# A fifth Winograd pair in blocks 3 to 6 of an attention and GEGLU kernel

## Chip, cores and metric

The kernel runs on one core of one Trainium2 chip. The metric is the device time of one launch, in microseconds; lower is better. The time before is the median of three runs.

## What is computed

The reference is linear attention followed by a gated feed-forward layer, in float32. With 8 batches, 8 heads, 576 positions and a head width of 64 it is, cut to what matters:

```python
q_s = softmax(q, axis=-1)                 # over the 64 of a head
k_s = softmax(k, axis=2)                  # over the 576 positions
kv  = einsum('bhsd,bhse->bhde', k_s, v)
x   = einsum('bhsd,bhde->bhse', q_s, kv)  # then heads side by side: 4608 x 512
g, val = x @ w_gate, x @ w_val            # 512 -> 1536 each
out = (gelu(g) * val) @ w_out             # 1536 -> 512
```

## The kernel before, in words

**Blocks.** The 576 rows of a batch are 512 main rows and 64 that are left over. Blocks 0 to 7 are the main rows of the eight batches; block 8 is the 8 x 64 left-over rows together. The order is 0 to 6, then 8, then 7. While block b runs through the feed-forward layer, the attention of block b+1 is fitted in, and loads go two blocks ahead. Tensors are float16 on TensorE; everything in PSUM is float32.

**Feed-forward of a block.** The hidden layer is twelve tiles of 128 columns, 0 to 11. A tile needs a gate and a value product: eight matmuls of 512 columns when done plainly. In the plain form (`half`) the steps are called `10g` and `10v`: after `g` ScalarE takes a Gelu of the PSUM bank (L625), after `v` VectorE multiplies it in (L627) and writes the tile of `ht`.

**Pairs.** From block 2 on, some tiles are computed in pairs k and k+3 with seven half-size products in place of eight (Winograd's form of Strassen's product): 28 matmuls of 256 columns for two tiles. `pair_step` cuts a pair into four steps, `k.1` to `k.4`, over three PSUM banks `pa`, `pb`, `pc`:

- `k.1`: product 1 into `pa`, which ScalarE copies to `pb` (L663); product 5 into `pc`, of which a scaled copy is taken (ScalarE L643; in blocks 7 and 8 VectorE L641).
- `k.2`: product 6 onto `pa`, of which ScalarE takes a copy (L643); product 3 onto `pc`; VectorE adds `pc` and the copy of `pa` into `cc` (L647).
- `k.3`: product 7 onto `pa`; VectorE adds `pa` and the copy of `pc` into `cc` (L647); product 2 onto `pb`, finished by `final` (ScalarE L633, VectorE L634); `upper` ends the other half: Gelu on ScalarE (L651), product on GpSimd (L653).
- `k.4`: product 4 onto `pa` and its `final`.

Since a product is put onto a bank in place, `k.2` on TensorE waits for the copies of `k.1`, `k.3` for the copy of `pa`, and `k.4` for the add of `pa` in `k.3`. A `final` is issued one pair step late where the next step is a `.1`. The buffer `cc` has two places, which the pairs take by turns from block 3 on.

**Sums.** The pairs need sums of weights (`sum_wgv`, L587, four for the gate and four for the value weights) and of x (`sum_x`, L593, GpSimd). The argument k = 6 of `sum_wgv` is pair 6, 7 is pair 7 and 8 is pair 8, and n says for how many pairs one instruction works; sum 3 is made in place. The output product is a Winograd product too (`out_strassen`, `product`, L718, seven products over tiles 0 to 5 and 6 to 11), with sums of `ht` (`sum_h`, L576): sums 1 to 4 for j = 0, 1, 2.

**Order.** Nothing reorders instructions; each engine follows the order that is written. For blocks 2 and up it is a string of steps: `THREE` for block 2, `FOUR` for blocks 3 to 6, `SIX` for 8 and 7. Letters run what the table `plan` holds under them (`ride`): `a`, `n`, `m` normalise q of the next block (VectorE L240 and L242, GpSimd L250), `l` loads, `t` is a DMA transpose, `s0`, `u0`, `s1`, `u1` are sums of `ht`, and `w`, `x` in block 2 are sums of weights. Step `2.4` comes inside `out_strassen`, after three tiles of its product 1. The points `NS` 0 to 4 in `out_strassen` run the attention of the next block, casts of v, and sums of weights. In this function VectorE also takes copies of PSUM (L750) and adds (L756).

Of the kernel before, what the change touches and what calls it, by code (L numbers as in the profile page):

```python
# [18 lines left out]
def kernel(  # L19
# [12 lines left out]
    B, H, S, D = q.shape  # L32
# [16 lines left out]
    NO = NFI // 2  # L49
# [30 lines left out]
    def big(shape, dt, name, hold=False, seed=False):  # L80
        tag = ring.pop(next(i for i, x in enumerate(ring) if x in full) if seed else 0)
        t = ps_big.tile(shape, dt, name=name, tag=tag)
        words = 1
        for n in shape[1:]:
            words *= n
        (full.add if words == 512 and shape[0] == 128 and dt == f32 else full.discard)(tag)
        if hold:
            held[id(t)] = (t, tag)
        else:
            ring.append(tag)  # L90
        return t

    def let_go(t):
        ring.append(held.pop(id(t))[1])
# [26 lines left out]
    for i, nm in enumerate("gv"):  # L121
        n = 3 * NO * P
# [472 lines left out]
    def product_gv(i, ps, xt, k, first):  # L595
# [3 lines left out]
        for t, w, nm in ((0, wv_sb, "v"), (1, wg_sb, "g")):  # L599
            ss = ws[(nm, k // NO)]  # L600
            for c in range(2):
# [7 lines left out]


    THREE = ("a 6g l 6v 0.1 9g 0.2 9v w 0.3 7g 0.4 n m 1.1 t 7v 1.2 10g 1.3 s0 10v 1.4 2.1 u0 8g 2.2 8v"
             " 2.3 s1 11g u1 2.4 11v x")
    FOUR = ("a 7g l 7v n 0.1 6.1 0.2 6.2 0.3 6.3 m 10g 0.4 6.4 1.1 t 10v 1.2 s0 8g u0 1.3 8v 1.4 2.1"
            " 11g s1 2.2 11v 2.3")
    SIX = ("0.1 6.1 0.2 6.2 0.3 6.3 0.4 1.1 6.4 7.1 s0 1.2 7.2 1.3 u0 7.3 1.4 2.1 7.4 8.1 2.2"
           " 8.2 2.3 s1 8.3 2.4")
    steps = {b: (SIX if b >= B - 1 else THREE if b == 2 else FOUR).split() for b in range(2, B + 1)}
    live = {}

    def half(b, xt, c, nm):  # L620
# [87 lines left out]
    def product(i, ps, first, ts=(0, 1), js=range(NO)):  # L708
        for j in js:
            for t in ts:  # L710
                c0, c1 = slice(t * P, (t + 1) * P), slice(256 + t * P, 256 + (t + 1) * P)
                a = {1: ht[:, j, c0], 2: ht[:, NO + j, c0], 3: s4[:, j, c0], 4: ht[:, NO + j, c1],
                     5: sh[1][:, j, c0], 6: sh[2][:, j, c0], 7: ht[:, j, c1]}[i]
                w = {1: wo_sb[:, j, 0:256], 2: wo_sb[:, NO + j, 0:256],
                     3: wo_sb[:, NO + j, 256:512]}.get(i)
                if w is None:
                    w = tw[{4: 4, 5: 1, 6: 2, 7: 3}[i]][:, j]
                nc.tensor.matmul(ps[t], a, w, start=(first and j == js[0] and (  # L718
                    t == ts[0] or ps[t].tensor is not ps[ts[0]].tensor)),
                                 stop=(j == js[-1]), skip_group_check=True)  # L720

    def get_x(b):
        return get_xt(b) if b < B else xtr

    def last_js(b):
        return (NO - 2 if b < 2 else NO // 2 - 1, NO)

    def out_strassen(b, last):
        yo = [yop.tile([P, 2, C], f32, name="yo", tag="yo") for _ in range(2)]
        c = (slice(0, 256), slice(256, 512))  # L730
        ps, tiles_ = {}, {}

        def get(nm):
            if last:
                tiles_[nm] = [big([P, 256], f32, "ps" + nm, True) for _ in range(2)]
                ps[nm] = [x for x in tiles_[nm]]
            else:
                tiles_[nm] = [big([P, 2, 256], f32, "ps" + nm, True)]
                ps[nm] = [tiles_[nm][0][:, t] for t in range(2)]

        def parts(nm):
            return [(0, ps[nm][0]), (1, ps[nm][1])] if last else [(slice(0, 2), tiles_[nm][0])]

        def snap(nm, act=False):
            sn = ffn.tile([P, 2, 256], f32, name="sn", tag="gl")
            for n, (t, src) in enumerate(parts(nm)):
                if n or act:
                    nc.scalar.activation(out=sn[:, t], in_=src, func=ACTF.Copy, scale=1.0 / _H_SCALE)
                else:
                    nc.vector.tensor_scalar(out=sn[:, t], in0=src, scalar1=1.0 / _H_SCALE,  # L750
                                            scalar2=None, op0=ALU.mult)
            return sn

        def add(nm, sn, half, col):
            for t, src in parts(nm):
                nc.vector.scalar_tensor_tensor(  # L756
                    out=yo[half][:, t, c[col]], in0=src, scalar=1.0 / _H_SCALE,
                    in1=sn[:, t], op0=ALU.mult, op1=ALU.add)

        js = (0, 1, 2, 3, 4, 5) if b < 2 else (0, 3, 1, 4, 2, 5)  # L760
        get("a")
        four = 2 < b < B - 1
        cut = 3 if four else 4
        product(1, ps["a"], True, js=js[:cut])
        if four:
            pair_step(b, get_x(b), NO // 2 - 1, 4)
            product(1, ps["a"], False, js=js[cut:4])
        ride(b, NS, 0)
        if four:
            ride(b, PR, "u1")  # L770
        if b >= B - 1:
            pair_step(b, get_x(b), NFI - NO // 2 - 1, 4)
        get("b")
        product(1, ps["a"], False, js=js[4:])
        if b > 1:
            s1 = snap("a", True)
        ride(b, PR, "e")
        sum_h(*last_js(b), (1,))
        if b >= B - 1:
            ride(b, PR, "u1")  # L780
        sum_h(*last_js(b), (2,))
        if b < 2:
            s1 = snap("a")
        product(2, ps["b"], True, js=js)
        add("b", s1, 0, 0)
        for x in tiles_["b"]:
            let_go(x)
        sum_h(*last_js(b), (4,), "pool" if b > 1 else "dve")
        get("c")
        product(5, ps["c"], True, js=js)  # L790
        sum_h(*last_js(b), (3,), "pool" if b > 1 else "dve")
        s5 = snap("c", b == B or b == B - 2)
        ride(b, NS, 1)
        product(6, ps["a"], False, js=js)
        s2 = snap("a", b == B or b == B - 2)
        ride(b, NS, 2)
        cut = NO - 1 if 1 < b < B - 2 else NO
        product(3, ps["c"], False, js=js[:cut])
        if cut < NO:
            product(7, ps["a"], False, js=js)  # L800
            add("a", s5, 1, 1)
            product(3, ps["c"], False, js=js[cut:])
        add("c", s2, 0, 1)
        for x in tiles_["c"]:
            let_go(x)
        store_rows(b, 0, yo[0])
        if last:
            finish_last(b, ps["a"], yo[1], s5)
            return
        if cut == NO:  # L810
            product(7, ps["a"], False, js=js)
            add("a", s5, 1, 1)
        ride(b, NS, 4)
        if b == B:
            go_on(B - 1, get_x(B - 1), 1)
        product(4, ps["a"], False, js=js)
        nc.scalar.activation(out=yo[1][:, :, c[0]], in_=tiles_["a"][0], func=ACTF.Copy,
                             scale=1.0 / _H_SCALE)
        let_go(tiles_["a"][0])
        store_rows(b, 1, yo[1])  # L820
# [97 lines left out]
    FI, NS, PR = range(3)  # L918
    plan = {}

    def at(b, kind, i, *fns):
        plan.setdefault((b, kind, i), []).extend(fns)

    L = lambda f, *a: (lambda: f(*a))
# [40 lines left out]
    for b in range(2, B):  # L965
        n = b + 1
# [13 lines left out]
    for b in range(2, B - 1):  # L980
        n = b + 1
# [6 lines left out]
    for b in range(2, B + 1):  # L988
        for j in range(NO // 2 - 1):
            at(b, PR, f"s{j}", L(sum_h, j, NO, (1,)))  # L990
            if j and b >= B - 1:
                at(b, PR, f"u{j}", L(sum_h, j, NO, (2, 3, 4)))
            else:
                at(b, PR, f"s{j}", L(sum_h, j, NO, (3,), "pool"))
                at(b, PR, f"u{j}", L(sum_h, j, NO, (2,)), L(sum_h, j, NO, (4,), "pool"))
    for i, xs_ in (("w", ("g1", "v1", "g2", "v2")), ("x", ("g4", "v4", "g3", "v3"))):
        for x in xs_:
            at(2, PR, i, L(sum_wgv, x[0], int(x[1]), NO, 1, "pool"))
    for b, i, x in ((3, 2, "g1"), (3, 2, "g2"), (4, 2, "v1"), (4, 2, "v2"), (6, 1, "g4"), (6, 1, "v4"),
                    (6, 2, "g3"), (6, 2, "v3")):  # L1000
        at(b, NS, i, L(sum_wgv, x[0], int(x[1]), NO + 1, 2))


    def ride(b, kind, i):
        for fn in plan.get((b, kind, i), []):
            fn()
# [63 lines left out]
```

## Time and profile before

| | |
|---|---|
| median of three runs | 293.6 us (293.58 to 293.72) |
| the profiled execution: time, span | 293.74 us, 292.0 us |
| TensorE busy | 282.8 us, 97% of the span |
| VectorE, ScalarE, GpSimd busy | 221.8, 194.9, 200.5 us |
| block 2 | 82.0 to 112.45 us of the span |
| blocks 3, 4, 5, 6 | 30.02, 30.08, 30.07, 30.28 us each |

The blocks are cut where the first matmul of a block's feed-forward part starts. The share of TensorE says that it is the engine to look at; whether it waits anywhere is read from its timeline. A row of the timeline has the start in us, the time, the engine, the line and operation, output and inputs, the count, and the wait ahead of it with what ended it. Instructions on ScalarE and VectorE overlap a little: the next one can start some 0.1 us ahead of the end that the row gives.

### The profile page before, as it was taken

The page shows a single profiled execution, that of the slowest core. Times are in us where ns is not written, and L with a number is a line of the kernel's source. Part 1 is how long each engine was busy: PE and PEld are TensorE (multiplying, and loading weights), DVE is VectorE, ACT ScalarE, POOL GpSimd, SP SyncE. Part 2 cuts the span into 40 slices and gives each one's busy share as a digit, 9 for nine tenths or more (in the row PEclk, how much of TensorE's full clock was granted, in tenths as well). Part 3 has the DMA queues.
Part 4 walks back from the last instruction along what each step waited for, and adds up shares of the span by engine and source line. Part 5 has one row for each costly group of instructions (what it writes and reads, how often), then busy time and mean ns, then how long its engine had stood idle before and what let it go on. Part 6 is the DMA issues. An engine that isn't in the chain of part 4 may idle for free.

```text
span 292.0 us, 6352 instructions
## 1 busy us (share of the span) xinstructions
PE 282.8 (97%) x2449; PEld 203.1 (70%) x2449; DVE 221.8 (76%) x412; ACT 194.9 (67%) x322; POOL 200.5 (69%) x187
## 2 busy tenths in 40 slices
PE   3999999999999999999999999999999999999994
PEld 1544446445866687778776878687868888888883
DVE  2854789878878768677967897687868879938992
ACT  3773367785786578758986798669864577537650
POOL 1567846970489799877888688869895576283640
PEclk9999999999999999999999999999999999999999
DMA  6999999998059704990299019901141110033003
GB/s 215 374 381 388 401 391 390 357 342 237 4 175 387 160 3 144 356 221 3 114 341 283 3 74 326 318 6 74 73 77 26 72 74 0 3 72 75 0 2 144
DMA packets 54622, 51.72 MB, mean 177 GB/s; under 512 B 18496, under 2 KB 50496, under 8 KB 54592
## 3 DMA queue, kind: packets, MB, share of 16 engines
q1 hardware_dynamic: 52864, 49.49, 53.5%
q10 hardware_dynamic: 1728, 1.84, 2.0%
q8 instruction: 19, 0.31, 0.4%
q14 instruction: 11, 0.09, 0.1%
HBM read 37.75 MB, written 9.44 MB: 162 GB/s over the span
## 4 chain that ended last, share of the span: by engine, by line
PE 94%; DVE 2%; DMA 2%; ACT 0%; issue 0%; ACTq 0%
PE pga L606 19%; PE psa L718 15%; PE psg L467 14%; PE psv L467 14%; PE pgc L606 9%; PE psc L718 7%; PE pgb L606 5%; PE psb L718 4%; PE psy L535 4%; DMA qt<-in_q_dram 2%; PE pskv L343 2%; PE psx L430 1%; DVE rq L240 1%; PE psx L409 1%; DVE eq L250 0%; PE pskv L284 0%
## 5 line engine op out<-in xcount | busy, mean ns | idle before, releaser
L467 PE MATMUL psg<-xt,wg_sb 128*128 128x512 f16 x184 | 49.3, 379 | 0.0
L467 PE MATMUL psv<-xt,wv_sb 128*128 128x512 f16 x184 | 49.2, 379 | 0.0
L250 POOL TENSOR_TENSOR eq<-eq,rrq 128x640 f16<-128x640 f16 (+1 forms) x27 | 34.7, 1303 | 11.8 <-DVE rrq L242 8.2
L718 PEld LDWEIGHTS <-ht 128*128 128x128 f16 x384 | 36.6, 98 | 7.6 <-issue 2.5
L606 PEld LDWEIGHTS <-wv_sb 128*128 128x128 f16 x248 | 24.1, 98 | 9.4 <-issue 1.0
L467 PEld LDWEIGHTS <-wv_sb 128*128 128x128 f16 x184 | 17.9, 98 | 18.0 <-issue 0.8
L653 POOL TENSOR_TENSOR ht<-eq 128x512 f16<-128x512 f32 x14 | 17.8, 1273 | 18.1 <-ACT eq L651 18.1
L467 PEld LDWEIGHTS <-wg_sb 128*128 128x128 f16 x184 | 17.9, 98 | 16.5
L576 POOL TENSOR_TENSOR s<-ht,sh 128x512 f16<-128x512 f16 x19 | 22.4, 1178 | 9.8 <-DVE sh L576 9.8
L634 DVE SCALAR_TENSOR_TENSOR ht<-pga,glq 128x256 f16<-128x256 f32 x31 | 13.1, 423 | 20.7 <-ACT glq L633 20.6
L188 POOL CAST v<-vt 128x640 f16<-128x640 f32 x26 | 18.7, 761 | 12.8 <-PE pskv L343 11.3
L576 POOL TENSOR_TENSOR ht<-ht 128x512 f16<-128x512 f16 x19 | 23.1, 1215 | 6.1 <-DVE sh L576 6.1
L606 PEld LDWEIGHTS <-wg_sb 128*128 128x128 f16 x248 | 24.2, 98 | 2.8
L653 POOL TENSOR_TENSOR ht<-cc 128x512 f16<-128x512 f32 x15 | 19.5, 1303 | 8.5 <-ACT cc L651 8.5
L472 ACT ACTIVATE gl<-psg 128x512 f32<-128x512 f32 x24 | 13.8, 598 | 16.7 <-PE psg L467 16.7
L633 ACT ACTIVATE glq<-pgb 128x256 f32<-128x256 f32 x31 | 11.7, 379 | 18.7 <-PE pgb L606 10.9
L718 PE MATMUL psa<-tw,ht 128*128 128x256 f16 x192 | 23.4, 272 | 0.1
L473 DVE SCALAR_TENSOR_TENSOR ht<-psv,gl 128x512 f16<-128x512 f32 x24 | 16.1, 688 | 9.5 <-PE psv L467 7.6
L212 ACT ACTIVATE ek<-kt 128x1280 f16<-128x1280 f32 (+1 forms) x11 | 19.1, 1748 | 5.5 <-DMA kt<-in_k_dram 3.9
L663 ACT COPY pgb<-pga 128x512 f32<-128x512 f32 x31 | 18.0, 580 | 6.7 <-PE pga L606 6.4
L643 ACT ACTIVATE snq<-pga 128x512 f32<-128x512 f32 x31 | 18.5, 600 | 4.0 <-PE pga L606 3.7
L240 DVE TENSOR_REDUCE rq<-eq 128x20 f32<-128x1280 f16 (+1 forms) x12 | 17.2, 1432 | 4.6 <-ACT eq L212 4.6
(172 smaller groups left out, 729.6 us busy)
## 6 DMA issues: line engine op xcount, KB each, us to landing
out_dram<-yo SPq DMA_DIRECT2D x15, 512.0 KB, 3.4
kt<-in_k_dram SPq DMA_DIRECT2D x7, 640.0 KB, 9.0
vt<-in_v_dram SPq DMA_DIRECT2D x7, 640.0 KB, 5.3
qt<-in_q_dram SPq DMA_DIRECT2D x7, 640.0 KB, 7.7
qt<-in_q_dram SPq DMA_DIRECT2D x8, 512.0 KB, 7.8
wost<-in_moe_w_out_dram SPq DMA_DIRECT2D x6, 512.0 KB, 7.9
kt<-in_k_dram SPq DMA_DIRECT2D x6, 512.0 KB, 9.5
vt<-in_v_dram SPq DMA_DIRECT2D x6, 512.0 KB, 5.8
```

What stands on the lines that cost most here:

```text
L188: nc.gpsimd.tensor_copy(out=dst, in_=src)
L212: nc.scalar.activation(out=dst[:, n0:NC, h0 * D:h1 * D].rearrange(o, d=D, **({"t": 2} if b >= QUAD else {})), in_=heads(tiles[(nm, b)], b, ...
L240: nc.vector.reduce_sum(rq, e, axis=mybir.AxisListType.X)
L250: (nc.gpsimd if eng == "pool" else nc.vector).tensor_tensor(out=e, in0=e, in1=rrq.unsqueeze(-1).to_broadcast((P, n, 2, D)), op=ALU.mult)
L467: nc.tensor.matmul(ps, w[:, ci, fi * P:(fi + 1) * P], xt[:, ci, :], start=(ci == 0), stop=(ci == HP - 1))
L473: nc.vector.scalar_tensor_tensor(out=ht[:, fi, :], in0=psv, scalar=_H_SCALE, in1=gl, op0=ALU.mult, op1=ALU.mult)
L576: (nc.gpsimd if eng == "pool" else nc.vector).tensor_tensor(out=o, in0=a, in1=b, op=op)
L606: nc.tensor.matmul(ps[:, t], a, x, start=(first and t == 0 and c == 0), stop=(c == 1), skip_group_check=True)
L643: nc.scalar.activation(out=sn, in_=ps, func=ACTF.Copy, scale=_H_SCALE)
L653: (nc.vector if k == NFI - NO // 2 - 1 else nc.gpsimd).tensor_tensor(out=ht[:, k:k + NO // 2 + 1:NO // 2, 256:512], in0=cc[:, :, 0], in1=c ...
L663: nc.scalar.copy(out=pb, in_=pa)
L718: nc.tensor.matmul(ps[t], a, w, start=(first and j == js[0] and (t == ts[0] or ps[t].tensor is not ps[ts[0]].tensor)), stop=(j == js[-1]), ...
```

## The change

Blocks 3 to 6 get pair 7, so tiles 7 and 10 are no longer done plainly in them; the string is now called `FIVE`, and pair 7 takes turns with pair 1. Tiles 8 and 11 stay plain. The sums of weights for pair 7, four for the gate and four for the value, are made together with those for pair 6 in block 2 (n = 2), on VectorE where it was GpSimd, four at `w` and two each at `NS` 1 and 2. The later sums, spread over blocks 3, 4, 5 and 6, are for pair 8 alone (n = 1). In blocks 3 to 6 the sums 2, 3 and 4 of `ht` for j = 1 are all on VectorE, in `out_strassen` behind sum 1 of j = 2; before, sum 3 was on GpSimd at `s1`, and sum 2 on VectorE and sum 4 on GpSimd stood ahead of bank `b`.

```diff
     THREE = ("a 6g l 6v 0.1 9g 0.2 9v w 0.3 7g 0.4 n m 1.1 t 7v 1.2 10g 1.3 s0 10v 1.4 2.1 u0 8g 2.2 8v"
-             " 2.3 s1 11g u1 2.4 11v x")
-    FOUR = ("a 7g l 7v n 0.1 6.1 0.2 6.2 0.3 6.3 m 10g 0.4 6.4 1.1 t 10v 1.2 s0 8g u0 1.3 8v 1.4 2.1"
-            " 11g s1 2.2 11v 2.3")
+             " 2.3 s1 11g u1 2.4 11v")
+    FIVE = ("a 8g l 8v n 0.1 6.1 0.2 6.2 0.3 6.3 m 0.4 1.1 6.4 7.1 t 1.2 s0 7.2 1.3 u0 7.3 2.1 1.4 11g 2.2"
+            " 7.4 s1 11v 2.3")
...
-        if four:
-            ride(b, PR, "u1")
...
         sum_h(*last_js(b), (1,))
-        if b >= B - 1:
+        if b > 2:
             ride(b, PR, "u1")
...
-            if j and b >= B - 1:
+            if j and b > 2:
                 at(b, PR, f"u{j}", L(sum_h, j, NO, (2, 3, 4)))
...
-    for i, xs_ in (("w", ("g1", "v1", "g2", "v2")), ("x", ("g4", "v4", "g3", "v3"))):
+    for kind, i, xs_ in ((PR, "w", ("g1", "v1", "g2", "v2")), (NS, 1, ("g4", "v4")), (NS, 2, ("g3", "v3"))):
         for x in xs_:
-            at(2, PR, i, L(sum_wgv, x[0], int(x[1]), NO, 1, "pool"))
-    for b, i, x in ((3, 2, "g1"), (3, 2, "g2"), (4, 2, "v1"), (4, 2, "v2"), (6, 1, "g4"), (6, 1, "v4"),
+            at(2, kind, i, L(sum_wgv, x[0], int(x[1]), NO, 2))
+    for b, i, x in ((3, 2, "g1"), (3, 2, "g2"), (4, 2, "v1"), (4, 2, "v2"), (5, 2, "g4"), (5, 2, "v4"),
                     (6, 2, "g3"), (6, 2, "v3")):
-        at(b, NS, i, L(sum_wgv, x[0], int(x[1]), NO + 1, 2))
+        at(b, NS, i, L(sum_wgv, x[0], int(x[1]), NO + 2, 1))
```

More of the change, by code (lines that the diff above doesn't have):

```diff
@@ L611 @@
     THREE = ("a 6g l 6v 0.1 9g 0.2 9v w 0.3 7g 0.4 n m 1.1 t 7v 1.2 10g 1.3 s0 10v 1.4 2.1 u0 8g 2.2 8v"
-             " 2.3 s1 11g u1 2.4 11v x")
-    FOUR = ("a 7g l 7v n 0.1 6.1 0.2 6.2 0.3 6.3 m 10g 0.4 6.4 1.1 t 10v 1.2 s0 8g u0 1.3 8v 1.4 2.1"
-            " 11g s1 2.2 11v 2.3")
+             " 2.3 s1 11g u1 2.4 11v")
+    FIVE = ("a 8g l 8v n 0.1 6.1 0.2 6.2 0.3 6.3 m 0.4 1.1 6.4 7.1 t 1.2 s0 7.2 1.3 u0 7.3 2.1 1.4 11g 2.2"
+            " 7.4 s1 11v 2.3")
     SIX = ("0.1 6.1 0.2 6.2 0.3 6.3 0.4 1.1 6.4 7.1 s0 1.2 7.2 1.3 u0 7.3 1.4 2.1 7.4 8.1 2.2"
            " 8.2 2.3 s1 8.3 2.4")
-    steps = {b: (SIX if b >= B - 1 else THREE if b == 2 else FOUR).split() for b in range(2, B + 1)}
+    steps = {b: (SIX if b >= B - 1 else THREE if b == 2 else FIVE).split() for b in range(2, B + 1)}
     live = {}
```

## The prediction, made before the result was known

> **What bounds the kernel now.** I read the page first (busy shares and the chain that ended last), then the busy time by block, then the timelines of block 2, of block 4 for the pairs and of block 8, which already runs pairs without a break.
>
> ```profile
> PE 282.8 (97%) x2449; PEld 203.1 (70%) x2449; DVE 221.8 (76%) x412; ACT 194.9 (67%) x322; POOL 200.5 (69%) x187
> PE 94%; DVE 2%; DMA 2%; ACT 0%; issue 0%; ACTq 0%
> ```
>
> TensorE is the bound: 94% of the chain. By block (columns: length, then the busy time of PE, weight loads, DVE, ACT, POOL):
>
> ```profile
> 82.00:112.45 30.45, 30.45 (x273) 21.72 (x272) 21.89 (x39) 21.51 (x35) 28.27 (x30) 1.00 0.52 156
> 142.47:172.55 30.08, 30.08 (x285) 23.04 (x284) 23.97 (x43) 23.53 (x41) 24.45 (x23) 1.00 0.61 180
> 232.90:261.50 28.60, 28.60 (x262) 25.29 (x261) 21.94 (x43) 17.18 (x36) 18.58 (x17) 1.00 0.10 31
> ```
>
> TensorE has no gap in any of them; the others are 70 to 93% busy, but they work in order and TensorE takes their results within a microsecond, so averages don't settle this change. In block 2 the place where `w` stands is tight (VectorE, then one TensorE and one GpSimd row):
>
> ```profile
> 87.22 0.69 DVE L627 SCALAR_TENSOR_TENSOR ht<-psv,gl 128x512 f16<-128x512 f32 x1
> 87.83 0.68 DVE L647 SCALAR_TENSOR_TENSOR cc<-pga,snq 128x512 f32<-128x512 f32 x1
> ...
> 88.76 0.38 PE L606 MATMUL pga<-xs,wv_sb 128*128 128x256 f16 x2
> ...
> 86.21 2.48 POOL L250 TENSOR_TENSOR eq<-eq,rrq 128x640 f16<-128x640 f16 x2
> ```
>
> The add of 0.3 ends at 88.51, and 0.4, which puts product 4 onto the same `pga`, starts at 88.76: 0.25 us of slack. What VectorE sums cost beside GpSimd (blocks 4 and 6):
>
> ```profile
> 164.52 1.26 POOL L576 TENSOR_TENSOR s<-ht,sh 128x512 f16<-128x512 f16 x1 [0.64 <-DVE sh L576]
> 164.81 1.26 DVE L576 TENSOR_TENSOR sh<-sh,ht 128x512 f16<-128x512 f16 x1
> ...
> 226.72 1.00 DVE L587 TENSOR_TENSOR kt<-wg_sb,kt 128x512 f16<-128x512 f16 x1
> 227.64 1.38 DVE L587 TENSOR_TENSOR kt<-wv_sb,kt 128x512 f16<-128x512 f16 x1
> 228.94 0.41 DVE L587 TENSOR_TENSOR wg_sb<-wg_sb 128x512 f16<-128x512 f16 x1
> ```
>
> The same sum takes 0.41 us alone and 0.8 to 1.4 us when GpSimd is at work: it ends 0.29 us after the GpSimd row (164.52 + 1.26 = 165.78; 164.81 + 1.26 = 166.07).
>
> **What the Trainium skill says.** "SBUF — State Buffer", Practical consequences: a VectorE instruction with two SBUF inputs contends with a GpSimd one that reads SBUF, and the loser is blocked, not slowed. The rows above agree. "ScalarE: Activation LUTs", What ACT_TABLE_LOAD costs: ACTIVATEs back to back overlap by about 93 ns. The trace agrees: the copies of 0.60 us follow each other every 0.49 us. I count spacings, not durations: ScalarE copy or snapshot 0.49, Gelu of 512 0.54 (from `cc`) or 0.50 (from PSUM), of 256 0.27; VectorE add or product from PSUM 0.60, L634 0.34, free sum 0.34. "TensorE: Matmul & The Clock Gate", section Wait — 56ns, not 53.3ns?: N / 2.4 GHz + 2.5 ns, so 215.8 ns for 512 columns; four take 0.865 us in the chain, 216 ns each, and four of 256 0.436 us, 109 ns.
>
> **The change, part by part.**
>
> *TensorE's saving.* Two plain tiles are 16 x 0.216 = 3.46 us, a pair 28 x 0.109 = 3.05 us: 0.41 us less in each of four blocks, **-1.64 us**, if nothing waits.
>
> *Block 2, `w` (g1, v1, g2, v2 on VectorE).* They stand behind L627 of 9v, so from 87.83. GpSimd's second L250 runs until 88.69: the first sum ends at about 88.98; three at 0.34 follow, and the add of 0.3 starts at 89.97 in place of 87.83 and ends at 90.65. Behind it on VectorE are the `final`s, the reduction at `n` and 7v's L627; who waits first is TensorE, whose 0.4 starts at 90.70, not 88.76. Cost **1.9 us**: 1.2 if all four are free (4 x 0.34 less the slack), 3.1 if each takes 0.82. TensorE is then late by as much as VectorE, so the rest of the block only shifts (1.4 needs its add at 95.80 and comes at 96.05).
>
> *Block 2, `NS` 1 and 2.* g4 and v4 stand between the copies of `psc` and `psa` (L750). In the times of before, VectorE is at 106.95; GpSimd, rid of its own weight sums, runs sum 3 of `ht` (106.7 to 107.9) and then the casts of v. As in block 6 each sum is blocked by one GpSimd row: g4 ends at 108.2, v4 at 109.2, the copy of `psa` at 109.85 in place of 108.34. Product 7 waits for that copy and was to start at 108.71: **1.2 us** (0 if both are free, 1.35 at block 6's 1.00 and 1.38). g3 and v3 follow up to 111.4; the add of `psa` can't start earlier anyway (product 7 ends at 111.4 now). Nothing more. GpSimd's 5.7 us (eight rows of 0.66 to 0.85) come free, but TensorE waited for none of them, and no DMA is issued or moved: 0.
>
> *Blocks 3 to 6, balance.* A pair against two plain tiles is ScalarE +1.6 us and VectorE +0.7 us by spacing; u1 adds two VectorE sums of 0.34, the smaller weight sums give 0.3 to 0.8 back. On average there is room (23.5 to 25.1, 24.0 to 24.9, of 29.7 us). It is a matter of order.
>
> *Blocks 3 to 6, order,* worked in the times of block 4. Up to 6.3 nothing changes (TensorE done at 149.30, ScalarE's last Gelu of 6.3 at 150.28). Then `FOUR` has 10g, 10v, 8g, 8v among the pair steps; `FIVE` has 0.4 1.1 6.4 7.1 1.2 7.2 1.3 7.3 2.1 1.4 in a row.
> 1. 0.4 needs the add of 0.3 (148.58 + 0.68 = 149.26): starts 149.32, +0.02. Then 1.1 at 149.77, 6.4 at 150.64, 7.1 at 151.08, 1.2 at 151.95, 7.2 at 152.82, and 1.3 is due at 153.72.
> 2. ScalarE in order: copy and snapshot of 1.1 150.82, 151.31; `final` 0.4 151.80; copy and snapshot of 7.1 152.07, 152.56; `final` 6.4 153.05; copy of `pga` for 1.2 153.32 to 153.92. So 1.3 starts at 153.97: **+0.25**.
> 3. VectorE: add of 1.2 153.97; s0 beside GpSimd's L250, 0.65; add of 7.2 155.22, of 1.3 155.82; L634 156.42; u0 156.76; add of 7.3 157.10 to 157.79. ScalarE's Gelu of 7.3 follows at 157.88, and only then the copy for 2.1, at 158.42 to 158.99.
> 4. 2.2, which waits for that copy, is due at 157.89 (7.3, 2.1, 1.4, 11g after 1.3) and starts at 159.04: **+1.15**.
> 5. ScalarE: snapshot of 2.1 158.91, `final` 1.4 159.40, 11g 159.67, copy for 2.2 160.17 to 160.77. VectorE: add of 2.2, L634 of 7.4, s1, 11v, add of 2.3: 160.82 + 0.60 + 0.34 + 0.34 + 0.60 + 0.68 = 163.38. Step 2.4 needs it and starts at 163.43.
> Before, 2.4 started at 161.85. So a block gets **1.6 us longer** (the 2.0 us of waits less the 0.41 saved and a wait of 0.15 at 156.26 that goes). I take 0.9 to 2.2, an error of 0.15 either way in each of the four waits. Below nothing would need all four gone.
>
> *Output of blocks 3 to 6.* Sum 1 of j = 2, u1 and sum 2 of j = 2 are five free sums, 1.7 us; before, from 164.02 to 165.99, three took 1.97, since GpSimd's sum 4 stood beside them. Block 8 has exactly these five at 0.34 each. Cost 0, covered by product 5; without the cover, up to 0.8 where GpSimd holds two of them. The moves of g4 and v4 from `NS` 1 of block 6 to `NS` 2 of block 5 lie beside products 7 and 3: 0. The four banks pairs 1 and 7 take beyond two are those that 8g, 8v and the `pc` and `pb` of pairs 0 and 6 have left by then: 0.
>
> Sum: -1.64 included, 4 x 1.6 + 1.9 + 1.2 = **+9.5 us** on the profiled 293.74 us (span 292.0 and 1.74 around it), so 303.2; the median stands 0.14 lower: **303.1 us**.
>
> **Rivals.**
> - *Pairs keep their pace.* Block 8 runs six pairs at 3.05 us with no gap. For: its order is nearly the same. Against: it takes the snapshot of `pc` on VectorE, has s0 ahead of the add of 1.2, and its 2.2 comes 4.36 us after its 1.3, not 3.92. Then only block 2 costs: 293.6 - 1.64 + 3.1 = 295.1 us. 8%.
> - *All hidden: faster.* One mechanism: VectorE gets ahead of `w` by some 2 us, so that the sums lie in its idle time (1.83 us before 86.61), and the pairs keep their pace. 293.6 - 1.64 = 292.0 us. It decides where VectorE's add of 0.3 ends before 88.7; the order puts the sums after that idle time, which speaks against. 4%.
> - *VectorE becomes the bound in the output too,* each of the four sums there blocked once (0.8 us a block) and `w` at 3.1: 303.1 + 3.2 + 1.2 = 307.5 us. 10%.
> - *The change doesn't do what it says:* the counts of L606 must rise by 112 and those of L467 fall by 64; a miss would leave the waits and no saving, 304.7 us. 1%.
>
> **How the numbers follow.** The forecast has 77%. Its own range is 4 x 0.9 + 1.2 + 0 = +4.8 to 4 x 2.2 + 3.1 + 1.35 = +13.2 at the extremes; both ends at once are unlikely, and with half of each it is 300.5 to 305.5. Reaching toward the neighbours: 298.6 to 306.3 us. A difference of 0.2% (0.6 us) is about what a measurement of this kernel can tell from no change. Faster 0.05, the same 0.02, slower 0.93.
>
> **What would show it.** TensorE waits in block 2 at 0.4 for L647 (about 1.9 us) and at product 7 for L750 (1.2 us); in each of blocks 3 to 6 at 2.2 for L663 (1.1), at 2.4 for L647 and at 1.3 for L643. Blocks 3 to 6 of 31.7 us and block 2 of 33.6. The prediction is wrong if blocks 3 to 6 stay near 29.7 us, or if 0.4 in block 2 starts within 0.5 us of the end of 7g.

## The result and the profile after

The changed kernel takes 304.45 us (median of four runs) against 293.66 us, 10.8 us more. Three of the four runs lie between 304.28 and 304.46 us; the fourth took 308.78 us, which lifts the ratio of the means to 1.0403 and makes its 95% interval wide (1.0311 to 1.0494); the medians alone give 1.037. The span of the profiled execution grew by 10.4 us, from 292.0 to 302.4.

The busy line of the page and the chain by engine, after:

```profile
PE 282.9 (94%) x2497; PEld 207.4 (69%) x2497; DVE 229.7 (76%) x436; ACT 200.6 (66%) x338; POOL 189.7 (63%) x175
PE 62%; ACT 14%; DVE 13%; issue 5%; DMA 3%; POOL 2%; ACTq 0%; DVEq 0%
```

TensorE was 94% of the chain before and is 62% now. The other engines have hardly more to do: ScalarE rose by 5.7 us, VectorE by 7.9, of which part is waiting for GpSimd inside sums, and GpSimd fell by 10.8. No engine became the bound; TensorE began to wait for two engines that are busy 76 and 66% of the time.

Busy time by block, after (blocks 2 to 6; the second number is the length):

```profile
81.82:114.65 32.83, 30.61 (x273) 21.81 (x272) 27.00 (x47) 21.52 (x35) 23.95 (x22) 1.00 0.47 145
114.65:146.24 31.59, 30.10 (x298) 24.11 (x296) 23.67 (x47) 24.69 (x43) 23.02 (x22) 1.00 0.55 167
146.24:177.88 31.64, 30.10 (x298) 24.10 (x296) 23.73 (x47) 24.90 (x45) 22.77 (x22) 1.00 0.55 172
177.88:211.47 33.59, 30.16 (x298) 24.19 (x296) 26.80 (x49) 25.90 (x44) 24.92 (x23) 1.00 0.52 157
211.47:243.33 31.86, 30.29 (x307) 24.33 (x305) 23.81 (x45) 19.28 (x41) 19.98 (x17) 1.00 0.24 73
```

Against before that is +2.38, +1.57, +1.56, +3.52 and +1.58 us. The sum is 10.6; the start is 0.18 earlier and blocks 8 and 7 are the same (59.07 against 59.10), which leaves the 10.4.

**Block 2, at `w`.** VectorE, then GpSimd's normalisation that runs into it, then TensorE's step 0.4:

```profile
87.66 1.15 DVE L587 TENSOR_TENSOR kt<-wg_sb 128x512 f16<-128x512 f16 x1
88.73 0.41 DVE L587 TENSOR_TENSOR kt<-wv_sb 128x512 f16<-128x512 f16 x1
...
89.74 0.68 DVE L647 SCALAR_TENSOR_TENSOR cc<-pga,snq 128x512 f32<-128x512 f32 x1
...
86.04 2.48 POOL L250 TENSOR_TENSOR eq<-eq,rrq 128x640 f16<-128x640 f16 x2
...
90.47 0.39 PE L606 MATMUL pga<-xs,wv_sb 128*128 128x256 f16 x2 [1.72 <-DVE cc L647]
```

The first sum is locked out: part of its 1.15 us is a wait for GpSimd's row, and it ends (88.81) 0.29 us after that row (88.52). The other three take 0.41. The add follows, and TensorE, due at 88.60 after 7g, starts 1.87 us late.

**Block 2, at `NS` 1.** The two sums ahead of the copy of `psa`, the copy, GpSimd's rows at that time, and product 7, which waits for the copy:

```profile
108.67 0.74 DVE L587 TENSOR_TENSOR kt<-wg_sb,kt 128x512 f16<-128x512 f16 x1
109.34 0.93 DVE L587 TENSOR_TENSOR kt<-wv_sb,kt 128x512 f16<-128x512 f16 x1
110.20 0.68 DVE L750 TENSOR_SCALAR sn<-psa 128x512 f32<-128x512 f32 x1
...
107.98 1.15 POOL L576 TENSOR_TENSOR ht<-ht 128x512 f16<-128x512 f16 x1
109.09 3.55 POOL L188 CAST v<-vt 128x640 f16<-128x640 f32 x4
...
110.93 1.47 PE L718 MATMUL psa<-tw,ht 128*128 128x256 f16 x12 [0.50 <-DVE sn L750]
```

Each sum is locked out by the rest of one GpSimd row: g4 ends (109.41) 0.28 us after the sum of `ht`, v4 (110.27) 0.27 us after the first of the four casts, which ends at 110.00.

**Block 4.** The three waits of TensorE, at 1.3, 2.2 and 2.4, then VectorE's add of 7.3, the Gelu behind it and the copy for 2.1 behind that, on ScalarE:

```profile
157.78 0.38 PE L606 MATMUL pga<-xs,wv_sb 128*128 128x256 f16 x2 [0.15 <-ACT snq L643]
...
162.78 0.38 PE L606 MATMUL pga<-xs,wsv 128*128 128x256 f16 x2 [0.92 <-ACT pgb L663]
...
167.19 0.38 PE L606 MATMUL pga<-xs,wv_sb 128*128 128x256 f16 x2 [0.47 <-DVE cc L647]
...
160.84 0.68 DVE L647 SCALAR_TENSOR_TENSOR eq<-pga,snq 128x512 f32<-128x512 f32 x1
...
161.61 0.63 ACT L651 ACTIVATE eq<-eq 128x512 f32<-128x512 f32 x1 [0.36 <-DVE eq L647]
162.15 0.58 ACT L663 COPY pgb<-pga 128x512 f32<-128x512 f32 x1
```

The last three rows and TensorE's 2.2 are one hand-over chain: add to 161.52, Gelu from 161.61, copy to 162.73, TensorE from 162.78. A bracket counts from the modelled end of the last matmul; from the time that the matmul was due the waits are 0.32, 1.08 and 0.63 us.

**Block 5** has a wait of its own, 1.62 us at product 4. VectorE, GpSimd, TensorE:

```profile
205.86 2.77 DVE L587 TENSOR_TENSOR kt<-wg_sb,kt 128x256 f16<-128x256 f16 x1
208.55 0.80 DVE L587 TENSOR_TENSOR kt<-wv_sb,kt 128x256 f16<-128x256 f16 x1
209.27 0.68 DVE L756 SCALAR_TENSOR_TENSOR yo<-psa,sn 128x512 f32<-128x512 f32 x1
...
205.46 1.04 POOL L274 TENSOR_TENSOR eq0r<-eq0r,rrq 64x512 f16<-64x512 f16 x1
206.45 2.76 POOL L188 CAST v<-vt 128x640 f16<-128x640 f32 x4
...
210.00 1.47 PE L718 MATMUL psa<-tw,ht 128*128 128x256 f16 x12 [1.62 <-DVE yo L756]
```

A sum of 256 columns took 2.77 us: it arrived while L274 ran and ended 0.14 us after the third of the four casts (208.63 against 208.49). The second sum and the add of `psa` stood behind it. A smaller part of block 5's extra time lies elsewhere: its 2.2 waits 1.20 us by the bracket, where block 4 has 0.92. There ScalarE's Gelu of 7.3 starts 0.37 us after the add has ended, in block 4 0.09; why is not settled.

### The profile page after: what moved, and what is told of

The parts are those of the page before. It is cut to its first block, busy times and chain, and to the rows that moved or that the text cites. A ratio compares the mean times of both kernels' runs of the same rounds, so it can differ in the third digit from the quotient of the medians.

```text
span 302.4 us, 6502 instructions
## 1 busy us (share of the span) xinstructions
PE 282.9 (94%) x2497; PEld 207.4 (69%) x2497; DVE 229.7 (76%) x436; ACT 200.6 (66%) x338; POOL 189.7 (63%) x175
## 4 chain that ended last, share of the span: by engine, by line
PE 62%; ACT 14%; DVE 13%; issue 5%; DMA 3%; POOL 2%; ACTq 0%; DVEq 0%
PE psa L718 11%; PE pga L606 11%; PE psg L467 9%; PE psv L467 9%; ACT snq L643 6%; PE psc L718 5%; PE pgc L606 4%; PE psy L535 3%; DVE cc L647 3%; PE psb L718 3%; DMA kt<-in_k_dram 3%; DVE eq L647 3%; ACT pgb L663 2%; PE pgb L606 2%; DVE kt L587 2%
## 5 line engine op out<-in xcount | busy, mean ns | idle before, releaser
L250 POOL TENSOR_TENSOR eq<-eq,rrq 128x640 f16<-128x640 f16 (+1 forms) x27 | 34.7, 1303 | 13.2 <-DVE rrq L242 8.9
L467 PE MATMUL psg<-xt,wg_sb 128*128 128x512 f16 x152 | 41.1, 379 | 0.0
L467 PE MATMUL psv<-xt,wv_sb 128*128 128x512 f16 x152 | 41.0, 379 | 0.0
L653 POOL TENSOR_TENSOR ht<-eq 128x512 f16<-128x512 f32 x16 | 20.4, 1272 | 24.6 <-ACT eq L651 24.6
L634 DVE SCALAR_TENSOR_TENSOR ht<-pga,glq 128x256 f16<-128x256 f32 x35 | 14.7, 421 | 23.7 <-ACT glq L633 23.5
L653 POOL TENSOR_TENSOR ht<-cc 128x512 f16<-128x512 f32 x17 | 21.8, 1279 | 14.6 <-ACT cc L651 14.6
L576 POOL TENSOR_TENSOR s<-ht,sh 128x512 f16<-128x512 f16 x15 | 17.3, 1153 | 14.5 <-DVE sh L576 14.5
L606 PE MATMUL pga<-xs,wv_sb 128*128 128x256 f16 x116 | 22.2, 273 | 4.2 <-DVE cc L647 2.7
L663 ACT COPY pgb<-pga 128x512 f32<-128x512 f32 x35 | 20.4, 584 | 5.3 <-PE pga L606 5.0
L606 PE MATMUL pga<-xs,wg_sb 128*128 128x256 f16 x116 | 22.1, 272 | 0.0
L643 ACT ACTIVATE snq<-pga 128x512 f32<-128x512 f32 x35 | 20.6, 605 | 2.3 <-PE pga L606 2.1
```

The source lines that it names most:

```text
L250: (nc.gpsimd if eng == "pool" else nc.vector).tensor_tensor(out=e, in0=e, in1=rrq.unsqueeze(-1).to_broadcast((P, n, 2, D)), op=ALU.mult)
L467: nc.tensor.matmul(ps, w[:, ci, fi * P:(fi + 1) * P], xt[:, ci, :], start=(ci == 0), stop=(ci == HP - 1))
L576: (nc.gpsimd if eng == "pool" else nc.vector).tensor_tensor(out=o, in0=a, in1=b, op=op)
L606: nc.tensor.matmul(ps[:, t], a, x, start=(first and t == 0 and c == 0), stop=(c == 1), skip_group_check=True)
L643: nc.scalar.activation(out=sn, in_=ps, func=ACTF.Copy, scale=_H_SCALE)
L653: (nc.vector if k == NFI - NO // 2 - 1 else nc.gpsimd).tensor_tensor(out=ht[:, k:k + NO // 2 + 1:NO // 2, 256:512], in0=cc[:, :, 0], in1=c ...
```

## The experiments

The theory: every microsecond is an order that lets an instruction stand in front of one that TensorE needs. The rivals: too much work on VectorE or ScalarE; a cost of the doubled sums wherever they stand. In the expectations, e2 is the kernel of "Pair 8's sums out of block 5", e3 that of "The order of the pairs alone" and e4 that with both diffs of "Inside the pair steps".

### The weight sums alone

The kernel before, with `FOUR` and the sums of `ht` untouched; only the weight sums are those of the change, in place, engine and n:

```diff
-            at(2, PR, i, L(sum_wgv, x[0], int(x[1]), NO, 1, "pool"))
+            at(2, kind, i, L(sum_wgv, x[0], int(x[1]), NO, 2))
...
-        at(b, NS, i, L(sum_wgv, x[0], int(x[1]), NO + 1, 2))
+        at(b, NS, i, L(sum_wgv, x[0], int(x[1]), NO + 2, 1))
```

> The order of blocks 3 to 6 and the sums of ht as before; only the places of the weight sums are those of the change (block 2 on VectorE, n = 2; pair 8 alone in blocks 3 to 6). Tile 10 is still done plainly in blocks 3 to 6, on weights into which sum 3 is already written, so its values are not those of the reference; the work is the same. If the waits of block 2 and block 5 belong to the sums: block 2 +2.4 us (step 0.4 about 1.9 late, product 7 about 0.6 late), block 5 +1.9 (product 4 late behind the sums of pair 8), blocks 3, 4, 6 unchanged: 297.9 us. Rival, the late pairs of block 5 put its sums beside the casts and the sums alone don't wait there: 296.0 us. Rival, the sums cost nothing without the fifth pair: 293.6 us.

Measured: 298.21 us, ratio 1.0154 (1.0139 to 1.0169). Block 2 is 32.94 us long, blocks 3 and 4 are 30.02 and 30.07, block 5 is 31.91. TensorE's waits, the three that the trace names in brackets:

```profile
90.84 0.39 PE L606 MATMUL pga<-xs,wv_sb 128*128 128x256 f16 x2 [1.73 <-DVE cc L647]
...
111.40 1.47 PE L718 MATMUL psa<-tw,ht 128*128 128x256 f16 x12 [0.60 <-DVE sn L750]
...
205.65 0.60 PE L718 MATMUL psa<-tw,ht 128*128 128x256 f16 x4 [1.78 <-DVE yo L756]
```

So 4.6 us of the 10.8 are the weight sums, without any fifth pair.

### Pair 8's sums out of block 5

```diff
-    for b, i, x in ((3, 2, "g1"), (3, 2, "g2"), (4, 2, "v1"), (4, 2, "v2"), (5, 2, "g4"), (5, 2, "v4"),
+    for b, i, x in ((3, 2, "g1"), (3, 2, "g2"), (4, 2, "v1"), (4, 2, "v2"), (6, 1, "g4"), (6, 1, "v4"),
```

> The changed kernel with pair 8's sums g4 and v4 taken out of block 5 (NS 2) and made in block 6 at NS 1, n = 1. If block 5's extra 2 us are these two sums, held up by GpSimd's casts ahead of the add that product 4 waits for: block 5 falls from 33.6 to 31.6 us like blocks 3 and 4, 302.4 to 302.6 us. Rival, block 5 is long for another reason (left-over rows of block 0, the loads): no change, 304.4 us; or the wait goes with the sums to block 6: 304.4 us with block 6 at 33.8.

Measured: 302.85 us, ratio 1.0312 (1.0297 to 1.0328), 1.6 us less than the changed kernel. Product 4 of block 5 no longer waits and block 6 has no new wait. The pair waits stay in every block, with 2.2 in block 5 at 1.20 where blocks 4 and 6 have 0.93. So block 5 is 31.91 us long and not the 31.6 that the expectation took, which is about the 0.25 us by which the time misses 302.4 to 302.6. The sums of pair 8 cost 1.6 us in block 5; the rest of its extra time is that wait.

### Pair 8's sums dealt out otherwise

```diff
-    for b, i, x in ((3, 2, "g1"), (3, 2, "g2"), (4, 2, "v1"), (4, 2, "v2"), (5, 2, "g4"), (5, 2, "v4"),
+    for b, i, x in ((3, 2, "g1"), (3, 2, "g2"), (4, 2, "g4"), (5, 2, "v1"), (5, 2, "v2"), (6, 1, "v4"),
```

> The changed kernel with pair 8's sums dealt out otherwise: g4 to block 4, v1 and v2 to block 5, v4 to block 6 (NS 1). In the changed kernel g4 took 2.77 us in block 5 and v1, v2 took 0.40 and 0.69 in block 4. If the place decides (block 5 has GpSimd's L274 ahead of the casts): v1 takes 2.5 us or more in block 5, product 4 waits 1.3 us or more there, g4 under 1 us in block 4: 304.2 us. If the form decides (sum 4 takes its second input from the sums' buffer): g4 takes 2 us or more in block 4, v1 and v2 under 1 us in block 5: 304.2 us with the wait in block 4, or less where the gap of block 4 takes it up, 302.7 us.

Measured: 304.48 us, with product 4 of block 5 waiting 1.62 us as before. g4 in block 4, then v1 in block 5, on VectorE:

```profile
173.93 0.40 DVE L587 TENSOR_TENSOR kt<-wg_sb,kt 128x256 f16<-128x256 f16 x1
...
205.91 2.77 DVE L587 TENSOR_TENSOR kt<-wv_sb 128x256 f16<-128x256 f16 x1
```

The place decides, not which sum it is.

### The left-over normalisation out of the way

```diff
-    at(5, NS, 1, norm_rem0)
+    at(5, PR, "m", norm_rem0)
```

> The changed kernel with the normalisation of the left-over rows of block 0 (VectorE L271 and L273, GpSimd L274) taken from NS 1 of block 5 to m. If pair 8's first sum waits 2.4 us in block 5 because it arrives while L274 runs and the casts of v follow that without a gap: with L274 gone it takes 0.4 to 0.9 us as in blocks 3 and 4, product 4 of block 5 doesn't wait, 302.5 to 302.8 us. Rival, the lock-out comes from the casts of block 5 alone: no change, 304.4 us.

Measured: 303.21 us, ratio 1.0326 (1.0309 to 1.0344). The two sums of block 5, with the same four casts beside them (205.96 to 208.80) but no L274 ahead:

```profile
206.43 0.40 DVE L587 TENSOR_TENSOR kt<-wg_sb,kt 128x256 f16<-128x256 f16 x1
206.75 0.80 DVE L587 TENSOR_TENSOR kt<-wv_sb,kt 128x256 f16<-128x256 f16 x1
```

The long sum is gone, and so is product 4's wait. (The edit also takes L271 and L273 from VectorE's queue there, so the sum now arrives 0.47 us into the first cast, not ahead of it.) The time is 0.4 us above what was expected since 2.2 of block 5 now waits 1.64 us where it was 1.20. The moved L274 causes that: it holds up GpSimd's next row, a sum of `ht` that now runs from 191.76 to 192.91. u0's sum on VectorE, which stands ahead of the add of 7.3, starts at 192.35, meets that row and takes 0.85 us in place of 0.41.

What is not settled is why the locked-out sum let three casts pass in block 5 when elsewhere it let one row pass.

### The order of the pairs alone

As in "Pair 8's sums out of block 5", and block 2's sums one at a time into VectorE's idle times, or on GpSimd:

```diff
-    THREE = ("a 6g l 6v 0.1 9g 0.2 9v w 0.3 7g 0.4 n m 1.1 t 7v 1.2 10g 1.3 s0 10v 1.4 2.1 u0 8g 2.2 8v"
-             " 2.3 s1 11g u1 2.4 11v")
+    THREE = ("a 6g l 6v 0.1 9g w1 0.2 9v 0.3 7g w2 0.4 n m 1.1 t 7v 1.2 10g 1.3 s0 10v w3 1.4 2.1 u0 8g w5 2.2 8v"
+             " 2.3 s1 11g u1 2.4 11v w4 x")
...
-    for kind, i, xs_ in ((PR, "w", ("g1", "v1", "g2", "v2")), (NS, 1, ("g4", "v4")), (NS, 2, ("g3", "v3"))):
+    for i, xs_, eng in (("w1", ("g1",), "dve"), ("w2", ("v1",), "dve"), ("w3", ("g2",), "dve"),
+                        ("w5", ("g3", "v3"), "pool"), ("w4", ("v2",), "dve"), ("x", ("g4", "v4"), "pool")):
         for x in xs_:
-            at(2, kind, i, L(sum_wgv, x[0], int(x[1]), NO, 2))
+            at(2, PR, i, L(sum_wgv, x[0], int(x[1]), NO, 2, eng))
```

> As e2, and block 2's weight sums spread: g1, v1, g2, v2 on VectorE one at a time into its idle times (after 9g, after 7g, after 10v, after 11v), g3 and v3 on GpSimd after 8g, g4 and v4 on GpSimd at x, all n = 2. If block 2's cost is only where the sums stand: block 2 back at 30.4 to 30.7 us, blocks 3 to 6 at 31.6 to 31.9: 293.6 + 4 x 1.57 = 299.9 us, up to 300.3. Rival, the doubled sums are too much for block 2 wherever they stand: block 2 still 1 us or more longer, 301 us or more. Rival, the waits of blocks 3 to 6 come from what block 2 leaves late: they fall too, below 298 us.

Measured: 300.87 us, ratio 1.0247 (1.0231 to 1.0262). Block 2 is 30.88 us, 2 us shorter than in the changed kernel. The doubled sums are all there, half of them on GpSimd, so it was where they stood that cost. A wait of 0.34 at product 3 is left: a sum of `ht` on VectorE, ahead of the copy of `psc`, is locked out by one of the weight sums that GpSimd makes at `x`, and takes 1.26 us. Block 3 is 31.59, as in the changed kernel: the pair waits don't depend on block 2. The time is 0.6 us above the expected 299.9 to 300.3, since block 2 keeps 0.4 us and 2.2 of block 5 waits 1.21.

### The sums of `ht` in the output alone

The kernel before with u1 as in the change, and nothing else:

```diff
-        if four:
-            ride(b, PR, "u1")
...
-        if b >= B - 1:
+        if b > 2:
             ride(b, PR, "u1")
...
-            if j and b >= B - 1:
+            if j and b > 2:
                 at(b, PR, f"u{j}", L(sum_h, j, NO, (2, 3, 4)))
```

> The kernel before with one part of the change: in blocks 3 to 6 the sums 2, 3 and 4 of ht for j = 1 all on VectorE, behind sum 1 of j = 2 in the output (weight sums and order of pairs as before). If five free sums cost no more than three of which one is locked out (1.7 against 1.97 us): no change, 293.4 to 293.9 us. Rival, two more sums a block on VectorE make the copy of psc or psa late: 0.3 us or more a block, 294.8 us or more.

Measured: 293.67 us, ratio 1.0006 (0.9977 to 1.0035). This part costs nothing that these runs can tell (the interval is about 0.9 us either way).

### Inside the pair steps: three edits

The first moves three copies a block from ScalarE to VectorE, the second only the order, the third, e4, does both; e4 ran before the other two. They start from the kernel of "The order of the pairs alone". Copies of `pc` to VectorE:

```diff
-            live[k] = [cc, pa, pb, pc, snap(pc, b >= B - 1)]
+            live[k] = [cc, pa, pb, pc, snap(pc, b >= B - 1 or (b > 2 and k in (1, 2, 7)))]
```

> As e3, with only the snapshots of pc of pairs 1, 7 and 2 moved from ScalarE to VectorE in blocks 3 to 6. If the wait at 1.3 is ScalarE's queue, it goes (0.3 to below 0.1); s0's sum then comes 0.6 us earlier, beside GpSimd's L250, and takes 1.4 us as in e4, so that 2.2 still waits about 1.0 and 2.4 about 0.2: blocks of 31.2 us, 299.3 us. Rival, VectorE simply has too much work (0.69 x 3 more a block): 302 us or more.

Sums of `ht` moved back:

```diff
-    FIVE = ("a 8g l 8v n 0.1 6.1 0.2 6.2 0.3 6.3 m 0.4 1.1 6.4 7.1 t 1.2 s0 7.2 1.3 u0 7.3 2.1 1.4 11g 2.2"
-            " 7.4 s1 11v 2.3")
+    FIVE = ("a 8g l 8v n 0.1 6.1 0.2 6.2 0.3 6.3 m 0.4 1.1 6.4 7.1 t 1.2 s0 7.2 1.3 7.3 u0 2.1 1.4 11g 2.2"
+            " 7.4 11v 2.3 s1")
```

> As e3, with only u0 moved behind 7.3 and s1 behind 2.3 in blocks 3 to 6; the copies stay on ScalarE. If 2.2 waits for VectorE's chain of adds and 2.4 for the add behind s1, each sum of 0.34 taken out of a chain shortens its wait by that: 2.2 about 0.7, 2.4 about 0.3, 1.3 still 0.3; blocks of 30.9 us, 298.1 us. Rival, ScalarE's queue is the whole of it: no change, 300.9 us.

Both of these diffs together:

> As e3, and in blocks 3 to 6 the snapshots of pc of pairs 1, 7 and 2 on VectorE, u0 after 7.3 and s1 after 2.3. If the waits at 1.3 and 2.2 are ScalarE's queue (seven instructions ahead of the copy for 1.2) and VectorE's chain of adds with the sums in between: 1.3 and 2.2 wait under 0.15 us each, 2.4 about 0.3; blocks of 29.7 to 30.1 us, 292.0 to 293.6 us in all. Rival, VectorE has too much work: three more copies of 0.69 us a block make the waits longer, 301 us or more.

Measured: 298.77 us (ratio 1.0171, 1.0157 to 1.0185), 298.36 us (1.0158, 1.0142 to 1.0173), and both 297.83 us (1.0140, 1.0123 to 1.0157), against 300.87 without. TensorE's 2.2 in block 4 in the first and the second:

```profile
160.42 0.38 PE L606 MATMUL pga<-xs,wsv 128*128 128x256 f16 x2 [1.01 <-ACT pgb L663]
```

```profile
159.95 0.38 PE L606 MATMUL pga<-xs,wsv 128*128 128x256 f16 x2 [0.59 <-ACT pgb L663]
```

With the copies on VectorE the named waits at 1.3 and 2.4 are gone and 2.2 is left; it waits 0.09 us more than the 0.92 it had without the edit. VectorE got three copies more in each block and the time fell by 2.1 us, so the amount of work on VectorE is not it. With the sums moved, every engine runs the same instructions and the time falls by 2.5 us: 1.3 still waits, 2.2 waits 0.33 less, the length of one sum, and 2.4's named wait is gone. For 1.3 the runs don't part the order on ScalarE from the amount of work there: its wait went only when ScalarE was rid of the copies. Both edits together fell far short of the expected 292.0 to 293.6: 2.2 waits 0.68 us and its second half another 0.22. The expectation missed that a sum which comes earlier meets another GpSimd row. In that run VectorE's s0 and GpSimd's L250 in block 4:

```profile
155.25 1.41 DVE L576 TENSOR_TENSOR sh<-ht 128x512 f16<-128x512 f16 x1
...
153.89 2.49 POOL L250 TENSOR_TENSOR eq<-eq,rrq 128x640 f16<-128x640 f16 x2
```

s0 stands between the add of 1.2 and the adds that 2.2 needs, and is locked out for 1.1 us. It took 1.41 us in the first of the three kernels too, and 0.63 in the second.

### No sum inside the chain

From the last kernel, with both edits in it; s0 and u0 now stand behind the adds, and three of block 2's sums stand elsewhere:

```diff
-    FIVE = ("a 8g l 8v n 0.1 6.1 0.2 6.2 0.3 6.3 m 0.4 1.1 6.4 7.1 t 1.2 s0 7.2 1.3 7.3 u0 2.1 1.4 11g 2.2"
+    FIVE = ("a 8g l 8v n 0.1 6.1 0.2 6.2 0.3 6.3 m 0.4 1.1 6.4 7.1 t 1.2 7.2 1.3 7.3 2.1 s0 1.4 11g u0 2.2"
             " 7.4 11v 2.3 s1")
...
-    THREE = ("a 6g l 6v 0.1 9g w1 0.2 9v 0.3 7g w2 0.4 n m 1.1 t 7v 1.2 10g 1.3 s0 10v w3 1.4 2.1 u0 8g w5 2.2 8v"
-             " 2.3 s1 11g u1 2.4 11v w4 x")
+    THREE = ("a 6g l 6v 0.1 9g w1 0.2 9v 0.3 7g w2 0.4 w6 n m 1.1 t 7v 1.2 10g 1.3 s0 10v w3 1.4 2.1 u0 8g w5 2.2 8v"
+             " 2.3 s1 11g u1 2.4 11v x")
...
-    for i, xs_, eng in (("w1", ("g1",), "dve"), ("w2", ("v1",), "dve"), ("w3", ("g2",), "dve"),
-                        ("w5", ("g3", "v3"), "pool"), ("w4", ("v2",), "dve"), ("x", ("g4", "v4"), "pool")):
+    for i, xs_, eng in (("w1", ("g1", "g2"), "dve"), ("w2", ("v1",), "dve"), ("w6", ("g4",), "pool"),
+                        ("w3", ("v2",), "dve"), ("w5", ("g3", "v3"), "pool"), ("x", ("v4",), "pool")):
```

> As e4, but s0 stands behind 2.1 and u0 behind 11g, so that no sum of ht stands between the adds of 1.2 and 7.3; in block 2 g2 goes beside g1, g4 to GpSimd after 0.4 and v2 after 10v. If what is left in e4 (2.2 waits 1.1 us) is s0's sum of 1.41 us, locked out by GpSimd's L250 in the middle of the chain, 2.2 waits under 0.15 and 2.4 under 0.2: blocks of 29.7 to 30.0 us, 292.3 to 293.5 us. Rival, the chain of copies, adds and Gelus is too long for five pairs without any sums in it: 2.2 still waits 0.5 us or more, 295.5 us or more.

Measured: **292.15 us, ratio 0.9945 (0.9933 to 0.9958)**, 1.6 us faster than the kernel before and a little below the expected 292.3 to 293.5. Blocks 2 to 6:

```profile
81.99:112.60 30.61, 30.44 (x273) 21.87 (x272) 26.62 (x43) 21.52 (x35) 28.34 (x26) 1.00 0.52 156
112.60:142.24 29.64, 29.64 (x298) 24.13 (x296) 26.11 (x50) 23.61 (x40) 23.39 (x22) 1.00 0.59 178
142.24:171.87 29.63, 29.63 (x297) 24.15 (x296) 26.15 (x50) 23.82 (x42) 23.17 (x22) 1.00 0.62 183
171.87:201.50 29.63, 29.63 (x297) 24.16 (x296) 25.85 (x50) 23.82 (x40) 24.51 (x23) 1.00 0.58 178
201.50:231.30 29.80, 29.77 (x306) 24.35 (x305) 26.62 (x50) 18.91 (x40) 21.02 (x18) 1.00 0.26 79
```

TensorE's busy time shows no gap in blocks 3 to 5. In blocks 3 and 4 VectorE is busier (26.1 us a block) than in the changed kernel (23.7), where it was waited for. From the kernel with both edits to this one the amount of work is the same and only places differ, and 5.7 us go.

## Why the prediction was right, point by point

- **TensorE's saving, 0.41 us a block: right.** The last version comes near to showing it bare: block 4 takes 29.63 us where it took 30.08. That is 0.41 by the count and the wait of 0.15 that went, less one of 0.09 that is left at 2.4.
- **Block 2 at `w`, 1.9 us at 0.4: right** (1.87). The first sum ended 0.29 us after the GpSimd row, as forecast: 88.98 in the times of before, 88.81 in a run whose block 2 starts 0.18 earlier. One figure in the working is off: 1.4, which started at 94.41 before, comes at 96.35 when 1.94 late, not at 96.05. Its add is in time either way; in the changed kernel 1.4 starts at 96.13 without a wait.
- **Block 2 at `NS` 1, 1.2 us at product 7: too large.** It was 0.66 (due at 110.27, started at 110.93). The wait was the right one, its size was not: I had GpSimd's sum 3 of `ht` end at 107.9, 0.95 us after VectorE is free for g4, and it ended 0.46 us after (109.13 against 108.67). GpSimd's rows there follow VectorE's sum 2 of j = 2. That sum took 0.77 us before, beside GpSimd's weight sums, and 0.42 with these gone; the forecast fits the 0.77. So g4 and v4 took 0.74 and 0.93, not 1.2 and 1.1, the copy came 0.7 us earlier than forecast, product 7 was due 0.2 us earlier, and block 2 got 2.38 us longer and not 3.1.
- **Blocks 3 to 6, 1.6 us each: right** for 3, 4 and 6 (1.57, 1.56, 1.58), and step by step: in block 4, 1.3 waits 0.32 (0.25 forecast), 2.2 1.08 (1.15), 2.4 0.63 (the remaining 0.6); blocks 3 and 6 have the same three waits to 0.05 us. The edits bear the chain out: the copies taken from ScalarE end the wait at 1.3, the sum u0 taken out from ahead of the add of 7.3 shortens 2.2 by 0.33, and with no sum ahead of that add 2.2 doesn't wait.
- **Block 5, sums of pair 8 beside products 7 and 3, 0: wrong.** Product 4 waited 1.6 us for them; a longer wait at 2.2, which stays when they are gone, makes up the rest of the 1.95 us by which block 5 exceeds block 4 (33.59 against 31.64). I had looked for the gap on VectorE (1.65 us ahead of the add of `psa` in block 5 of before) and not at what GpSimd does in it: L274 and then the casts. Looking there would not have been enough: with one GpSimd row for each sum, as elsewhere in the forecast, both sums would have ended by about 207.3, ahead of the add of `psa`, which product 7 allows at about 207.6 (an estimate from the rows of block 5). That a sum lets three casts pass is what the forecast didn't have.
- **The output's sums, 0: right.** The part alone gives 1.0006, and in the changed kernel the five sums take 0.41 to 0.42 us each in every one of blocks 3 to 6.
- The two misses have opposite signs, -0.7 and +1.95, and that they partly cancel is luck. With them the forecast +9.5 becomes +10.7; the five blocks grew by 10.6, the span by 10.4, the median by 10.8. The range narrowed by half should have read 300.8 to 305.0, not 300.5 to 305.5; 304.45 lies in both.
- The rivals: the pairs did not keep their pace, nothing of `w` was hidden, the sums of `ht` in the output were not locked out, and VectorE's load was not the cause. Open are why 2.2 of block 5 waits 0.28 us longer, and whether 1.3 could be cured by order alone.

## What to carry to other kernels

When a bound engine takes results within a microsecond, replay the queues of the helper engines instruction by instruction through the new order; the busy shares, 76 and 67% before, didn't show it here. What is put into such a queue delays the next instruction that the bound engine needs by its length, less the slack there, so place sums that nobody waits for behind that instruction. For every VectorE sum with two inputs in SBUF, look up what GpSimd runs at that very time, and what is queued behind that.

## What the hardware showed unexpectedly

A VectorE sum of 128x256, a size that takes 0.28 us when free (sum 3 in block 6 of the last version), took 2.77 us when it arrived while GpSimd's L274 ran with casts queued behind it, in two kernels with different sums (2.94 us in the one with the weight sums alone). It let L274 and three casts, 0.7 us each, pass. With L274 moved away it took 0.40 us beside the same casts. Elsewhere a locked-out sum let one GpSimd row pass (1.15 us at `w`, 1.41 us at s0), even where the same casts were queued behind that row (g4 in block 2, 0.74 us). What decides between the two is not known from these runs.
